# One-core transformer block: query-weight sums one per attention iteration, seventh product half an iteration earlier, GpSimd sums in halves, weight versions loaded ahead

## The chip, the cores and the metric

The kernel runs on one core of a Trainium2 chip. The metric is the device time of one execution in microseconds (us); lower is better. Each run was marked fast or slow; slow is here one more than 1.5% above the fastest of its kernel. Ratios and their 95% intervals use fast runs alone. Kernels that were sent together ran on the same chip, with the kernel before among them. Kernels on different chips are compared by their ratios to the kernel before.

The engines, as the profile names them: PE is TensorE, PEld its weight loads, DVE is VectorE, ACT is ScalarE, POOL is GpSimd, SP is SyncE. A name with a q at its end (ACTq, SPq) is the sequencer of that engine when it issues DMA transfers. L273 is a line of the kernel's source; lines shift by a few between versions of the kernel.

## The reference

One block on 2048 tokens of width 1024: adaptive layer norm, grouped-query attention with 32 query heads of 128 on 512 cached keys, output projection, layer norm again, and a SwiGLU feed-forward part (FFN) of width 3584.

```python
def _A_ref(x, k_cache, v_cache, wq, wo):
    q = (x @ wq).reshape(B, Sq, Hq, Dh) ...          # 32 heads of 128
    k, v = ... the last 512 keys and values, each shared by 8 heads
    p = _softmax(einsum('bhqd,bhkd->bhqk', q, k) * Dh ** -0.5)
    return einsum('bhqk,bhkd->bhqd', p, v) ... @ wo
def _B_ref(x, w_gate, w_up, w_down):
    return _silu(x @ w_gate) * (x @ w_up) @ w_down
mod = _silu(c) @ w_mod                               # six modulation rows
h = _layernorm(x) * (1 + ca) + sa
x = x + ga * _A_ref(h, k_cache, v_cache, wq, wo)
h = _layernorm(x) * (1 + cb) + sb
return x + gb * _B_ref(h, w_gate, w_up, w_down)
```

## The kernel before

The tokens are worked off in two stages of 1024: attention of stage one, its output projection, attention of stage two, its output projection, then the FFN of each stage. The large matrix products are done with a seven-product scheme for 2x2 blocks (seven block products instead of eight). It spares TensorE one eighth of the work and needs sums of weight blocks instead. Three engines share what that brings:

- The sums of the query weights are made on VectorE, four sums of 128x512 for each group of four attention iterations.
- The sums of all other weights are made once, by GpSimd, in 58 "units" (16 for the output projection, 28 for gate and up, 14 for down). A unit loads 512 KB, makes four sums, and writes the result to DRAM. It works in one of two slots of SBUF, at 131 KB and 138 KB.
- The output and down projections later load whole "versions" of their weights, in the order of the seven products. Those loads are issued from ScalarE's queue.

```python
def sum_ops(self, st, eng):              # four sums of one group of weights
    T.op(st, lambda: eng.tensor_tensor(s1, a21, a22, ADD), ...);  yield
    T.op(st, lambda: eng.tensor_tensor(s2, s1, a11, SUB), ...);   yield
    T.op(st, lambda: eng.tensor_tensor(s4, a12, s2, SUB), ...);   yield
    T.op(st, lambda: eng.tensor_tensor(s3, a11, a21, SUB), ...);  yield

def wq_tick(sc, i):
    ...                                  # load of the group's weights
    if (i + 5) % 4 == 0 and 0 <= hp < HP:
        wq_of[sc, hp].sums(DVE, V)       # all four sums, one after the other

def unit_tick(i):                        # GpSimd: one unit every three iterations
    if i % 3 == 0:
        unit_step(OFF_ST if i % NI < NI - 8 else OFF_ST[1:])
```

An attention iteration handles one head and 512 tokens. It has up to two of the seven query products, four score products, two exponentials on ScalarE, and 16 value products, which VectorE evicts from PSUM (L803 takes the reciprocal, L806 multiplies). There are 64 iterations in a stage (`NI`).

```python
def attend(sc, lo, pre, tick):
    hi = (sc + 1) * NI
    for i in range(lo, hi + 2):
        pre(i)
        turn = i % 4 == 2 and group_at(sc, i - 2) >= 0 and i < hi
        if not turn:
            q_first_half(sc, i)
        if lo <= i - 1 < hi:
            scores(i - 1)                # 4 products, 2 exponentials (ACT L784)
        if turn:
            q_first_half(sc, i)          # the fourth product, copied by ACT L1010
        if sc * NI <= i - 2 < hi:
            pv(i - 2)                    # 16 products, eviction DVE L803 and L806
        q_second_half(sc, i)
        tick(i)                          # wq_tick, unit_tick
        ...
        if i == hi - 6:
            start_o(sc)                  # first version of the output weights
        ...
def o_phase(sc, hook):
    load, ver = wo0[sc]
    load(1)                              # second version, after all of attention
    ...
```

The softmax here doesn't subtract the row's maximum and nothing guards it: scores larger than these inputs give would overflow.

## Time and profile before

| | before |
|---|---|
| median, lowest to highest of 4 runs | 1256.13 us, 1253.12 to 1257.26 |
| span of the profiled execution | 1265.0 us |
| PE busy | 1179.5 us, 93% |
| attention iteration, mean of the two loops (24th to 63rd and 65th to 127th eviction) | 3.9 us |
| PE's waits for the eviction L806 | 42.7 us in 21 waits |

From the profile page of the kernel before: the busy time of each engine, the clock that TensorE was granted in 40 slices (in tenths), and the engines of the chain of waits that ended last.

```profile
span 1265.0 us, 18135 instructions
PE 1179.5 (93%) x7087; PEld 589.4 (47%) x7087; DVE 784.5 (62%) x1297; ACT 525.4 (42%) x735; POOL 392.2 (31%) x423
...
PE 79%; DVE 12%; DMA 5%; issue 2%; ACT 2%; POOL 0%; ACTq 0%; DVEq 0%; POOLq 0%
```

TensorE bounds the kernel, and VectorE is the engine that it waits for. The view of waits, for PE of the kernel before, says for what (the line waited for, us in total, number of waits, longest):

```profile
PE ps L273 <- DVE arena L806: 42.7, 21, 5.3
PE ps L273 <- ACT arena L1010: 8.5, 21, 0.5
PE ps L273 <- DMA arena<-in_A_wo_dram: 7.9, 2, 4.2
PE ps L273 <- DMA arena<-in_B_w_down_dram: 5.1, 3, 2.6
```

Nearly two thirds of what is shown is one cause. The view in order of time of the kernel before shows two bursts of the four query-weight sums; the first meets GpSimd sums only from 496.20 on, the second meets one at each. Columns: start, duration, engine, line, operation, output and input, count, and in brackets the idle time before it with what ended it.

```profile
495.15 0.41 DVE L878 TENSOR_TENSOR arena<-arena 128x512 f16<-128x512 bf16 x1
495.60 0.42 DVE L880 TENSOR_TENSOR arena<-arena 128x512 f16<-128x512 f16 x1
...
509.48 1.22 POOL L880 TENSOR_TENSOR arena<-arena 128x512 f16<-128x512 f16 x1
509.72 1.26 DVE L880 TENSOR_TENSOR arena<-arena 128x512 f16<-128x512 f16 x1
...
511.01 2.04 DVE L882 TENSOR_TENSOR arena<-arena 128x512 f16<-128x512 bf16 x1
511.60 1.17 POOL L882 TENSOR_TENSOR arena<-arena 128x512 f16<-128x512 bf16 x1
512.85 1.22 POOL L884 TENSOR_TENSOR arena<-arena 128x512 f16<-128x512 bf16 x1
513.09 1.26 DVE L884 TENSOR_TENSOR arena<-arena 128x512 f16<-128x512 bf16 x1
...
515.07 0.69 DVE L806 TENSOR_TENSOR arena<-ps,rl 128x512 f16<-128x512 f32 x1
...
515.82 4.91 PE L273 MATMUL ps<-arena 128*128 128x129 bf16 x26 [2.50 <-DVE arena L806]
```

The first three sums of the first burst take 0.41 and 0.42 us. The first of the second burst, which begins in the last 0.44 us of a GpSimd sum, takes 0.72 us, and the four that run beside GpSimd sums take 1.26 to 2.04 us (the longest of all 104 takes 3.35 us, L878). The sum begun at 511.01 ends at 513.05, 0.28 us after the GpSimd sum of 511.60 to 512.77. How the two engines hinder each other the trace does not show; it shows the times. The four sums stand in VectorE's queue ahead of the eviction, so the eviction begins at 515.07 and PE has waited 2.50 us. The groups of the kernel before, VectorE's lines by shape, give the mean over all 26 bursts (us busy, mean ns):

```profile
L882 DVE TENSOR_TENSOR arena<-arena 128x512 f16<-128x512 bf16 x26 | 27.9, 1075 | 0.9
L880 DVE TENSOR_TENSOR arena<-arena 128x512 f16<-128x512 f16 x26 | 24.4, 940 | 0.9
...
L884 DVE TENSOR_TENSOR arena<-arena 128x512 f16<-128x512 bf16 x26 | 20.1, 774 | 0.9
L878 DVE TENSOR_TENSOR arena<-arena 128x512 f16<-128x512 bf16 x26 | 17.9, 689 | 0.0
```

That is 90.3 us for 104 sums, 0.87 us each. After a stall the trace also shows a lower clock. The table by stretch of the kernel before (us, then busy time and count of PE, PEld, DVE, ACT and POOL, then the granted clock, the DMA share and GB/s):

```profile
480.00:485.00 5.00, 2.81 (x28) 1.61 (x26) 4.31 (x5) 2.66 (x4) 4.46 (x5) 1.00 0.73 203
485.00:490.00 5.00, 5.00 (x29) 2.32 (x26) 1.56 (x3) 3.17 (x5) 3.66 (x4) 0.66 0.74 193
```

PE idles 2.19 us in the first stretch, in a wait that ends at 484.44, and in the next it is busy all the time at a clock of 0.66, with 29 products instead of the 46 of the stretch after. The 0.66 is an average: the clock stood at 0.50 from 485.57 to 488.99, 3.41 us. The wait of 2.50 us that ends at 515.82 is followed in the same way, by a clock of 0.50 from 516.29 to 519.70. That the low clock comes from the idleness is read from this order and not tested. Seven such pieces lie in the two attention loops of the kernel before (24th to 63rd and 65th to 127th eviction), and each costs up to 1.7 us, so up to 12 us in all (estimates, 3.41 us at half speed).

### The profile page before, as it was taken

How to read it: one execution, taken by the hardware profiler on the slowest of the kernel's cores; microseconds unless marked ns; L12 is line 12 of the kernel's file. 1: busy time of each engine (PE TensorE's matmuls, PEld its weight loads, DVE VectorE, ACT ScalarE, POOL GpSimd, SP SyncE). 2: the span in 40 equal slices, each digit the busy share in tenths (PEclk: the TensorE clock that was granted, in tenths of full speed). 3: DMA queues.
4: the chain of work that ended last, by engine and by line, in shares of the span. 5: the costliest groups of instructions: out<-in, count | busy, mean ns of one | idle time of the engine just before them, and what ended most of it. 6: DMA issues, size and time to landing. Idle time of an engine off the chain costs nothing.

```text
span 1265.0 us, 18135 instructions
## 1 busy us (share of the span) xinstructions
PE 1179.5 (93%) x7087; PEld 589.4 (47%) x7087; DVE 784.5 (62%) x1297; ACT 525.4 (42%) x735; POOL 392.2 (31%) x423
## 2 busy tenths in 40 slices
PE   8798988898998889889889999999999999999998
PEld 5465555453444545445444444444444444444343
DVE  4857776646686776675548766654555654554445
ACT  4475666650105666657620124454401154444110
POOL 1470667533204676775344004443000000000000
PEclk9899999998999999999999999999999999999999
DMA  9786678798845779985789847687397466452453
GB/s 330 190 202 152 177 185 195 170 201 212 248 114 120 180 180 189 207 212 138 179 212 233 237 154 244 215 263 232 115 257 194 138 199 200 152 181 91 160 187 104
DMA packets 305861, 238.71 MB, mean 189 GB/s; under 512 B 132208, under 2 KB 279664, under 8 KB 305776
## 3 DMA queue, kind: packets, MB, share of 16 engines
q1 hardware_dynamic: 234800, 121.67, 39.1%
q0 software_dynamic: 16704, 60.82, 15.9%
q10 hardware_dynamic: 54272, 55.05, 14.3%
q8 instruction: 56, 0.92, 0.3%
q14 instruction: 29, 0.24, 0.1%
HBM read 172.49 MB, written 34.60 MB: 164 GB/s over the span
## 4 chain that ended last, share of the span: by engine, by line
PE 79%; DVE 12%; DMA 5%; issue 2%; ACT 2%; POOL 0%; ACTq 0%; DVEq 0%; POOLq 0%
PE ps L273 78%; DVE arena L806 2%; DMA arena<-in_A_wo_dram 2%; DMA arena<-in_B_w_down_dram 2%; DVE arena L882 2%; DVE arena L880 1%; DVE arena L814 1%; ACT arena L1010 1%; DVE arena L878 1%; ACT arena L784 1%; DVE st L414 1%; DVE arena L594 1%; DVE rl L803 1%; DMA arena<-in_B_w_gate_dram 0%; DVE arena L433 0%
## 5 line engine op out<-in xcount | busy, mean ns | idle before, releaser
L273 PE MATMUL ps<-arena 128*128 128x512 f16 (+3 forms) x6782 | 1172.4, 335 | 80.9 <-DVE arena L806 42.7
L273 PEld LDWEIGHTS ps<-arena 128*128 128x128 bf16 (+1 forms) x6782 | 579.4, 99 | 666.7 <-DVE arena L806 56.0
L784 ACT ACTIVATE arena<-ps 128x1024 bf16<-128x1024 f32 x256 | 261.1, 1022 | 72.4 <-PE ps L273 60.4
L817 ACT ACTIVATE tmp<-ps 128x512 f32<-128x512 f32 x166 | 99.1, 597 | 387.6 <-PE ps L273 332.9
L814 DVE TENSOR_TENSOR arena<-ps,tmp 128x512 bf16<-128x512 f32 (+1 forms) x134 | 91.8, 685 | 59.8 <-PE ps L273 57.1
L814 DVE TENSOR_TENSOR arena<-ps,nsc 128x512 f16<-128x512 f32 x84 | 57.8, 688 | 80.5 <-PE ps L273 68.1
L803 DVE RECIPROCAL rl<-ps 128x4 f32<-128x4 f32 x128 | 23.0, 180 | 122.0 <-PE ps L273 121.5
L806 DVE TENSOR_TENSOR arena<-ps,rl 128x512 f16<-128x512 f32 x128 | 88.5, 691 | 4.9 <-DVE rl L803 0.5
L817 ACT ACTIVATE nsc<-ps 128x512 f32<-128x512 f32 x84 | 50.1, 597 | 96.2 <-PE ps L273 93.8
L1051 DVE TENSOR_TENSOR arena<-arena 128x2048 f16<-128x2048 f16 (+3 forms) x56 | 59.6, 1074 | 18.3 <-PE ps L273 17.7
L419 POOL TENSOR_SCALAR rstd<-mv 128x1 f32<-128x1 f32 x28 | 6.3, 225 | 205.0 <-DVE mv L418 178.8
L1473 ACT ACTIVATE arena<-arena 128x512 f16<-128x512 f16 x84 | 49.8, 624 | 30.7 <-DVE arena L814 30.7
L941 POOL TENSOR_TENSOR arena<-arena 128x512 f16<-128x512 bf16 x30 | 35.8, 1192 | 86.2 <-DMA arena<-in_B_w_down_dram 70.4
L878 POOL TENSOR_TENSOR arena<-arena 128x512 f16<-128x512 bf16 x28 | 34.2, 1220 | 68.9 <-DMA arena<-in_B_w_up_dram 35.1
L817 ACT ACTIVATE arena<-ps 128x512 f32<-128x512 f32 x16 | 9.6, 597 | 90.5 <-PE ps L273 90.5
L814 DVE TENSOR_TENSOR tmp<-ps,tmp 128x512 f32<-128x512 f32 x32 | 22.0, 688 | 38.4 <-ACT tmp L817 28.8
L414 DVE BATCH_NORM_STATS2 st<-x_res 128x6 f32<-128x512 bf16 x62 | 42.3, 682 | 4.0 <-DMA x_res<-in_A_x_dram 3.6
L1490 DVE TENSOR_TENSOR arena<-ps,arena 128x512 f16<-128x512 f32 x28 | 19.4, 692 | 37.1 <-PE ps L273 37.1
L428 DVE TENSOR_SCALAR nsc<-x_res,mv,rstd 128x1024 f16<-128x1024 bf16 (+1 forms) x30 | 20.6, 686 | 29.0 <-DMA arena<-nsc 27.8
L945 POOL TENSOR_TENSOR arena<-arena 128x512 f16<-128x512 bf16 x30 | 37.2, 1241 | 1.5
L943 POOL TENSOR_TENSOR arena<-arena 128x512 f16<-128x512 bf16 x30 | 36.9, 1231 | 2.4
L594 DVE SCALAR_TENSOR_TENSOR arena<-arena 128x1024 bf16<-128x1024 bf16 x24 | 37.5, 1560 | 0.0
(94 smaller groups left out, 700.4 us busy)
## 6 DMA issues: line engine op xcount, KB each, us to landing
arena<-wgu_sum SPq DMA_DIRECT2D x56, 512.0 KB, 6.9
arena<-in_A_wq_dram SPq DMA_DIRECT2D x28, 512.0 KB, 4.8
wgu_sum<-arena POOLq DMA_DIRECT2D x28, 512.0 KB, 3.8
arena<-wo_sum ACTq DMA_DIRECT2D x7, 2048.0 KB, 10.2
arena<-in_B_w_gate_dram SPq DMA_DIRECT2D x28, 512.0 KB, 4.2
arena<-in_B_w_up_dram SPq DMA_DIRECT2D x28, 512.0 KB, 6.4
arena<-wd_sum ACTq DMA_DIRECT2D x8, 1792.0 KB, 8.3
arena<-in_B_w_down_dram ACTq DMA_DIRECT2D x6, 1792.0 KB, 8.3
```

Source lines behind the costliest of these rows:

```text
L273: T.op(PE, lambda: TE.matmul(out_ap, lhsT, rhs, start=start, stop=stop, skip_group_check=skip), reads=reads, writes=[bank_buf])
L414: T.op(DVE, lambda: V.bn_stats(st_[sl][:, hf * 6:hf * 6 + 6], x_res[:, t, hf * 512:hf * 512 + 512]), reads=[B_x[t]], writes=[B_st[sl]])
L594: T.op(DVE, lambda: V.scalar_tensor_tensor(mt[n % 2], mt[n % 2], 1.0, sc_row, op0=ALU.mult, op1=ALU.mult, accum_out=mcol[:, n:n + 1]), rea ...
L784: T.op(ACT, lambda: A.activation(ex_s[es][:, 2 * kp:2 * kp + 2, :], banks2(SCB + 2 * kp), AF.Exp, scale=att_scale), writes=[PB[SCB + 2 * k ...
L806: T.op(DVE, lambda: V.tensor_tensor(o_s[os_].rearrange("p (a b) d -> p a b d", a=2), psap(PVB * 512, [[512, 2], [130, 2], [1, P]]), rlb, A ...
L814: T.op(DVE, lambda: V.tensor_tensor(out, bank(ba), other, ADD), reads=[ob2], writes=[PB[ba], ob])
L817: T.op(ACT, lambda: A.activation(dst, bank(bk), AF.Copy), writes=[PB[bk], db])
L878: T.op(st, lambda: eng.tensor_tensor(s1, a21, a22, ADD), reads=[R, self.b_s3], writes=[self.b_s[0]])
L943: T.op(POOL, lambda: g.tensor_tensor(e[1], b22, e[0], SUB), reads=[R, w.b_s[0]], writes=[w.b_s[1]])
L945: T.op(POOL, lambda: g.tensor_tensor(e[2], b21, e[1], SUB), reads=[R, w.b_s[1]], writes=[w.b_s[2]])
L1051: T.op(DVE, lambda: V.tensor_tensor(o, a, b, SUB), reads=rd, writes=[sb])
L1473: T.op(ACT, lambda: A.activation(o, s_, AF.Silu), reads=[sb], writes=[ob])
```

## The change

Its intent is to take the bursts apart, shorten what VectorE must wait for, and start weight loads before they are missed. In full:

1. The four query-weight sums are made one per iteration.
2. The seventh product moves half an iteration up and takes the place before the scores; the fourth product goes ahead of the scores as well, so its copy on ScalarE stands before the exponentials.
3. GpSimd makes each sum in two halves of 128x256.
4. GpSimd's units come two per five iterations (0.40 an iteration instead of 0.33), and their last ones earlier.
5. The rest of version one and all of version two of the output weights are loaded in the last iteration but one of attention, no longer after it. To have room, they lie partly in GpSimd's two unit slots (131 to 145 KB). The down weights' first versions are loaded one round earlier.
6. Statistics and input loads move to other iterations.

```diff
+def sum_ops(self, st, eng, parts=1):
+    for (o, a, b, op, rd, wr) in (...the four sums...):
+        for h in range(parts):
+            T.op(st, lambda: eng.tensor_tensor(...part h of parts...))
+        yield
 ...                                         # in unit_sums
-    yield from w.sum_ops(POOL, g)
+    yield from w.sum_ops(POOL, g, 2)        # likewise for the other units
 ...
 def q_first_half(sc, i):                    # c = i % 4
-    ...products 3, 2, 4, 5 for c = 0, 1, 2, 3
+    ...products 3, 7, 4, 5
 def q_second_half(sc, i):
-    ...products 7, 1, 6 for c = 1, 2, 3
+    ...products 2, 1, 6
 ...                                         # in wq_tick
-    hp = group_at(sc, i + 5)
-    if (i + 5) % 4 == 0 and 0 <= hp < HP:
-        wq_of[sc, hp].sums(DVE, V)
+    hp = group_at(sc, i + 4 - i % 4)
+    if 0 <= hp < HP and (sc, hp) in wq_of:
+        if i % 4 == 0:
+            sums_of[sc, hp] = wq_of[sc, hp].sum_ops(DVE, V)
+        if (sc, hp) in sums_of:
+            next(sums_of[sc, hp])
 def unit_tick(i):
-    if i % 3 == 0:
-        unit_step(OFF_ST if i % NI < NI - 8 else OFF_ST[1:])
+    if i % 5 in (0, 2):
+        unit_step(OFF_ST if i % NI < NI - 14 else OFF_ST[1:])
 ...                                         # in tick0, likewise in stage two
-    if 6 <= i < NI - 3:
+    if 6 <= i < NI - 8:
         unit_tick(i)
 ...                                         # in start_o
-    places = [[(OFF_WQ, 14), (136 * KB, 2)], [(OFF_E, HP)]] + ...
+    places = [[(OFF_WQ, 14), (131 * KB, 2)], [(133 * KB, 12), (OFF_E, 4)]] + ...
-    wo0[sc][0](0)
+    wo0[sc][0](0, (0,))
 ...                                         # in attend
+    if i == hi - 1:
+        wo0[sc][0](0, (1,))
+        wo0[sc][0](1)
 ...                                         # in o_phase
-    load(1)
 ...                                         # in o_units
-    if j == 1 and (sc or idx % 2 == 0):
+    if j == 1 and idx > 1 and (sc or idx % 2 == 0):
 ...                                         # in the FFN
-    if r == FP - 1:
+    if r == FP - 2:
         ...load(0)
+    if r == FP - 1:
+        load(1)
```

More of the change, by code (lines that the diff above doesn't have):

```diff
@@ L870, in sums @@
                         pass
-                def sum_ops(self, st, eng):
+                def sum_ops(self, st, eng, parts=1):
                     r, (s1, s2, s4) = self.raw, self.s
-                    a11, a12 = r[:, 0:HK, 0:P], r[:, HK:DT, 0:P]
-                    a21, a22 = r[:, 0:HK, P:2 * P], r[:, HK:DT, P:2 * P]
-                    s3 = self.s3
-                    R = self.b_raw
-                    T.op(st, lambda: eng.tensor_tensor(s1, a21, a22, ADD), reads=[R, self.b_s3], writes=[self.b_s[0]])
-                    yield
-                    T.op(st, lambda: eng.tensor_tensor(s2, s1, a11, SUB), reads=[R, self.b_s[0]], writes=[self.b_s[1]])
-                    yield
-                    T.op(st, lambda: eng.tensor_tensor(s4, a12, s2, SUB), reads=[R, self.b_s[1], self.b_s3], writes=[self.b_s[2]])
-                    yield
-                    T.op(st, lambda: eng.tensor_tensor(s3, a11, a21, SUB), reads=[R], writes=[self.b_s3])
-                    yield
+                    R, n = self.b_raw, HK // parts
+                    for (o, a, b, op, rd, wr) in ((s1, (0, P), (HK, P), ADD, [R, self.b_s3], self.b_s[0]),
+                                                  (s2, s1, (0, 0), SUB, [R, self.b_s[0]], self.b_s[1]),
+                                                  (s4, (HK, 0), s2, SUB, [R, self.b_s[1], self.b_s3], self.b_s[2]),
+                                                  (self.s3, (0, 0), (0, P), SUB, [R], self.b_s3)):
+                        for h in range(parts):
+                            x, y = [r[:, z[0] + h * n:z[0] + h * n + n, z[1]:z[1] + P] if type(z) is tuple else z[:, h * n:h * n + n, :]
+                                    for z in (a, b)]
+                            T.op(st, lambda: eng.tensor_tensor(o[:, h * n:h * n + n, :], x, y, op), reads=rd, writes=[wr])
+                        yield
             def seven_at(off, name, kind):
@@ L940, in unit_sums @@
                 R = w.b_raw
-                T.op(POOL, lambda: g.tensor_tensor(e[0], b12, b11, SUB), reads=[R, w.b_s3], writes=[w.b_s[0]])
-                yield
-                T.op(POOL, lambda: g.tensor_tensor(e[1], b22, e[0], SUB), reads=[R, w.b_s[0]], writes=[w.b_s[1]])
-                yield
-                T.op(POOL, lambda: g.tensor_tensor(e[2], b21, e[1], SUB), reads=[R, w.b_s[1]], writes=[w.b_s[2]])
-                yield
-                T.op(POOL, lambda: g.tensor_tensor(rf[:, 1536:2048], b22, b12, SUB), reads=[R], writes=[w.b_s3])
-                yield
+                for (o, a, b, rd, wr) in ((e[0], b12, b11, [R, w.b_s3], w.b_s[0]), (e[1], b22, e[0], [R, w.b_s[0]], w.b_s[1]),
+                                          (e[2], b21, e[1], [R, w.b_s[1]], w.b_s[2]), (rf[:, 1536:2048], b22, b12, [R], w.b_s3)):
+                    for h in range(2):
+                        c = slice(256 * h, 256 * h + 256)
+                        T.op(POOL, lambda: g.tensor_tensor(o[:, c], a[:, c], b[:, c], SUB), reads=rd, writes=[wr])
+                    yield
             def unit_write(k):
@@ L1018, in q_first_half @@
                 c = i % 4
-                if c == 0:
-                    q_step(sc, group_at(sc, i), 3)
-                elif c == 1:
-                    q_step(sc, group_at(sc, i + 3), 2)
-                elif c == 2:
-                    q_step(sc, group_at(sc, i - 2), 4)
+                if c < 3:
+                    q_step(sc, group_at(sc, i - c), (3, 7, 4)[c])
                 else:
@@ L1029, in q_second_half @@
                 c = i % 4
-                if c == 1:
-                    q_step(sc, group_at(sc, i - 1), 7)
-                elif c == 2:
-                    q_step(sc, group_at(sc, i + 2), 1)
-                elif c == 3:
-                    q_step(sc, group_at(sc, i + 1), 6)
+                if c > 0:
+                    q_step(sc, group_at(sc, i + 4 - c), (2, 1, 6)[c - 1])
             ORDER = (1, 2, 6, 5, 3, 7, 4)
@@ L1143, in loader, with load @@
                 got = {}
-                def load(idx):
+                def load(idx, which=None):
                     n = ORDER[idx]
                     dt = BF16 if n < 4 else F16
-                    got[idx], k0 = [], 0
+                    k0 = 0
+                    got.setdefault(idx, [])
                     for q, (off, m) in enumerate(places[idx]):
+                        if which is not None and q not in which:
+                            k0 += m
+                            continue
                         b_ = _Buf("%sv%d_%d_%d" % (kind, sc, idx, q))
@@ L1184, in run_x @@
                         bgx.pop(0)
-            LOADX = {8: 2, 16: 3}
+            LOADX = {6: 2, 12: 3}
             LOADT = {14 + 4 * n: n for n in range(NL)}
@@ L1190, in _ @@
             late = {}
+            sums_of = {}
             def wq_tick(sc, i):
@@ L1256, in pre0 @@
                 mods(i)
-                if i == 20:
+                if i == 14:
                     bg.append(stats_task(2 * TPC, 2 * TPC))
@@ L1270, in start_o @@
                 two = [(103 * KB, 7), (117 * KB, 9)] if sc == 0 else [(OFF_E, HP)]
-                places = [[(OFF_WQ, 14), (136 * KB, 2)], [(OFF_E, HP)]] + [[(o, HP)] for o in (OFF_WQ, OFF_E, OFF_WQ, OFF_N)] + [two]
+                places = [[(OFF_WQ, 14), (131 * KB, 2)], [(133 * KB, 12), (OFF_E, 4)]] + [[(o, HP)] for o in (OFF_WQ, OFF_E, OFF_WQ, OFF_N)] + [two]
                 wo0[sc] = loader(sc, A_wo, wo_sum, HP, "o", places)
-                wo0[sc][0](0)
+                wo0[sc][0](0, (0,))
             def attend(sc, lo, pre, tick):
@@ L1278, in attend @@
                     pre(i)
-                    turn = i % 4 == 2 and group_at(sc, i - 2) >= 0 and i < hi
-                    if not turn:
-                        q_first_half(sc, i)
+                    q_first_half(sc, i)
                     if lo <= i - 1 < hi:
                         scores(i - 1)
-                    if turn:
-                        q_first_half(sc, i)
                     if sc * NI <= i - 2 < hi:
@@ L1292, in attend @@
                         start_o(sc)
+                    if i == hi - 1:
+                        wo0[sc][0](0, (1,))
+                        wo0[sc][0](1)
                     if i >= hi - 1:
                         n = 5 * (i - hi + 1)
-                        o_early(sc, 0, n, n + 5)
-                        o_early(sc, 1, n, n + 5)
+                        for j in range(2):
+                            o_early(sc, j, n, min(n + 5, 14))
             AB_O = (QB, XB, PVB, PVB + 1)
@@ L1316, in o_phase @@
                 load, ver = wo0[sc]
-                load(1)
                 n1 = _N1()
-                b_sj = [_Buf("sj%d" % j) for j in range(TPC)]
-                offs = [(128 + 2 * j) * KB for j in range(TPC)]
-                sj = [(arena.at(offs[j], [CH], F32, [b_sj[j]]), b_sj[j]) for j in range(TPC)]
+                sj = []
                 def rings(tt, j, half):
@@ L1330, in hk @@
                         load(idx + 2)
+                    if j == TPC - 1 and idx == 2:
+                        for n in range(TPC):
+                            b_ = _Buf("sj%d" % n)
+                            sj.append((arena.at((128 + 2 * n) * KB, [CH], F32, [b_]), b_))
                     hook(idx, j)
-                seven_products(HP, oT, B_oT, OFF_OT, n1, ver, AB_O, BB_O, o_out(sc, sj, rings), sj, True, hk, (15, 15, 0, 0))
+                seven_products(HP, oT, B_oT, OFF_OT, n1, ver, AB_O, BB_O, o_out(sc, sj, rings), sj, True, hk, (14, 14, 0, 0))
             def o_units(sc, idx, j):
-                if j == 1 and (sc or idx % 2 == 0):
+                if j == 1 and idx > 1 and (sc or idx % 2 == 0):
                     unit_step(OFF_ST[1:])
@@ L1375, in pre1 @@
             def pre1(i):
-                if i == NI:
+                if i == NI + 46:
                     bg.append(stats_task(0, 2 * TPC))
@@ L1384, in tick1 @@
                     wq_tick(1, i)
-                    if i < 2 * NI - 3:
+                    if i < 2 * NI - 8:
                         unit_tick(i)
@@ L1580, in _ @@
                         load(0)
+                    if r == FP - 1:
+                        load(1)
                 if sc == 0:
                     take_w(FP)
-                load(1)
                 b_sj = [_Buf("fj%d_%d" % (sc, j)) for j in range(TPC)]
```

## The prediction

The forecast's sum: 35 us from attention and 8 to 9 us from the loads, about 44 us, and 1256 less 44 is the 1212 us predicted.

> **What bounds the kernel now.** TensorE. The page gives it 1179.5 of 1265 us busy, and the chain of waits is 79% PE, 12% VectorE, 5% DMA. The stretch table shows where the missing 85 us lie: FFN and output projections run at 93-99% busy; the two attention stages (about 60-282 and 392-643 us) leave 20 and 30 us idle. PE's waits there are mostly for VectorE's attention eviction L806 (15.5 and 21.9 us), which releases the value-product banks. The time-ordered view shows why: once per four iterations VectorE runs the four query-weight sums back to back ahead of that eviction. Each sum takes 0.42 us alone but 1.26 to 2.05 us beside a GpSimd sum (1.15-1.25 us); a burst is 1.7-5.3 us against about 2.5 us of slack. [...]
>
> A second loss: in 5-us stretches that follow such stalls the granted clock is 0.66-0.75 (about eight stretches, estimate 13 us lost). [...]
>
> Elsewhere: each output projection waits 3.7-4.2 us for the second weight version, which can be loaded only when the exponential buffers are free; the down projections wait about 2.5 us twice, and 1 us.
>
> **What the change does.**
> 1. One sum per iteration, after the eviction: no burst, at most 1.3 us between evictions. VectorE has room: 2.6 us an iteration against 3.9. An undisturbed iteration is, by durations in the trace, 1.51 (query products) + 0.86 (scores) + 1.0-1.06 (values) = 3.4 us. Ideal attention: about 30 us less in the second, 18 in the first, clock loss included.
> 2. GpSimd halves: 8 x about 0.6-0.65 us (estimate from half of 1.15 plus a fixed part) instead of 4 x 1.2: [...] VectorE sums average perhaps 0.7 us instead of 0.87.
> 3. Seventh product half an iteration earlier: QB's reader is done before the fourth product, whose ScalarE copy goes ahead of the exponentials; removes the 0.4-us waits for L1010 (8.5 us in all).
> 4. Statistics moved to where VectorE is less loaded.
> 5. Version loads earlier: up to 3.7+4.2 in the output projections and 5-6 us in the FFN, all on the chain.
>
> Ceiling about 50 + 13 = 63 us. I take 70% of attention (35) and 65% of the loads (8-9), about 44 us. Unchanged: the h-sums stall near 111 us (5 us), start (13 us), tail.
>
> **Predicted 1212 us, range 1194 to 1236.** Faster by over 2%: 0.80; within 2%: 0.18; slower: 0.02.
>
> **What would show it.** PE busy share 95-97%; waits for L806 from 42.7 to under 15 us; L878-L884-type VectorE means fall to 0.6-0.75 us; 5-us stretches with clock below 0.8 in attention nearly gone; attention stages near 205-210 and 220-228 us; PE waits for the output and down weights under 5 us together; GpSimd halves 0.55-0.7 us. PE waits on L1010 under 3 us.
>
> **What would make it wrong.** Units come at 0.4 an iteration instead of 0.33, one per 8.6 us, about GpSimd's free pace (8-9 us, 15 with one slot). If it lags, the early load of version two, which needs both unit slots, holds ScalarE's queue before the last exponentials and costs 5-10 us per attention stage. ScalarE (2.7 us an iteration) may become the next limit. In iterations with a modulation column (1.2-1.6 us) VectorE may still be late.

## The result, and the profile after

| | before | change |
|---|---|---|
| median, lowest to highest of 4 runs | 1256.13 us, 1253.12 to 1257.26 | 1220.89 us, 1218.16 to 1225.01 |
| ratio of the fast runs | | 0.9726, 95% interval 0.9694 to 0.9758 |
| span of the profiled execution | 1265.0 us | 1223.2 us |

A ratio is the mean time of one kernel's fast runs over that of the other's fast runs of the same rounds, so it is not quite the ratio of the medians quoted. The change is faster by 35 us of median. The two profiled executions differ by 41.8 us, because that of the kernel before happened to be slower than its median; the ledger below is in those.

The page of the change, the lines that answer to those of before:

```profile
span 1223.2 us, 18300 instructions
PE 1154.5 (94%) x7002; PEld 591.4 (48%) x7087; DVE 735.3 (60%) x1297; ACT 527.9 (43%) x735; POOL 452.8 (37%) x655
...
PE 60%; DMA 16%; POOL 15%; DVE 4%; issue 3%; ACT 1%; ACTq 0%; POOLq 0%; DVEq 0%; SPq 0%
```

VectorE has left the chain (12% to 4%), and GpSimd with its DMA transfers has come onto it: 15% and 16%, where they had 0% and 5%. PE's waits in the change:

```profile
PE ps L273 <- ACT arena L784: 31.0, 5, 18.3
PE ps L273 <- DVE arena L806: 10.7, 2, 5.8
```

The waits for the eviction are down from 42.7 to 10.7 us; those for L1010, the output weights and the down weights are gone. In their place stand 31.0 us of waits for the exponentials L784, where there had been 2.0. Two of the five make up nearly all of it. The groups of the change, by shape, VectorE's query-weight sums and GpSimd's halves:

```profile
L882 DVE TENSOR_TENSOR arena<-arena 128x512 f16<-128x512 bf16 x78 | 42.9, 550 | 0.1
L882 DVE TENSOR_TENSOR arena<-arena 128x512 f16<-128x512 f16 x26 | 13.3, 512 | 0.1
...
L943 POOL TENSOR_TENSOR arena<-arena 128x256 f16<-128x256 bf16 x240 | 176.3, 740 | 92.3 <-DMA arena<-in_B_w_down_dram 70.4 <-DMA arena<-in_A_wo_dram 8.6
```

The 104 sums of VectorE take 56.2 us, 0.54 us each. A half takes GpSimd 0.74 us, so two take 1.48 us where a whole sum took about 1.2.

The table by stretch of the change, same columns as before: a long undisturbed part of attention of stage two, and one stretch at its end.

```profile
390.95:522.19 131.24, 130.19 (x1061) 79.29 (x1080) 86.03 (x173) 102.55 (x121) 91.16 (x124) 1.00 1.02 199
...
595.00:600.00 5.00, 0.00 (x0) 0.00 (x0) 0.00 (x0) 0.00 (x0) 4.52 (x7) 0.50 0.08 28
```

The first covers 40 iterations, 3.28 us each, with PE busy 99% at full clock. In the second nothing runs but GpSimd. Here is the view in order of time of the change at the end of attention of stage one:

```profile
255.41 15.25 ACTq L1144 DMA_DIRECT2D arena<-in_A_wo_dram  x3
...
260.22 5.89 POOL L882 TENSOR_TENSOR arena<-arena 128x256 f16<-128x256 bf16 x8 [5.50 <-DMA arena<-in_B_w_up_dram]
266.40 0.57 POOL L950 DMA_DIRECT2D wgu_sum<-arena  x1 [0.30 <-POOL arena L882]
270.72 2.14 ACT L784 ACTIVATE arena<-ps 128x1024 bf16<-128x1024 f32 x2 [14.38 <-issue]
...
272.91 1.91 PE L273 MATMUL ps<-arena 128*128 128x129 bf16 x16 [10.95 <-ACT arena L784]
```

Read it from the bottom. PE waits 10.95 us for the last two exponentials. These wait 14.38 us, put down to "issue": ScalarE waits for nothing of its own. Ahead of them in its queue are the three loads L1144 that the change put there; they occupy the queue from 255.41 to 270.66, because their place in SBUF is GpSimd's slots, and GpSimd's last unit is summed at 260.22 and its write begins at 266.40. The exponentials begin at 270.72, 0.06 us after the loads have left the queue: here a load that waited for room held the arithmetic behind it. At the end of stage two the same pattern holds PE for 18.34 us (the loads at 593.25 for 12.15 us, the last unit's sums at 595.09, the exponentials at 605.45). There the clock is 0.50 from 591.33 to 611.81.

A ledger, in start times of the eviction L806 (it has one per iteration), before and after:

| part | before, us | change, us | difference |
|---|---|---|---|
| start to 4th eviction | 48.42 | 49.80 | +1.4 |
| 4th to 24th | 79.94 | 83.12 | +3.2 |
| 24th to 63rd | 150.59 | 127.14 | -23.5 |
| 63rd to 64th (end of attention one) | 3.07 | 15.02 | +12.0 |
| 64th to 65th (output projection one) | 111.23 | 106.25 | -5.0 |
| 65th to 127th | 246.99 | 206.07 | -40.9 |
| 127th to 128th (end of attention two) | 3.06 | 22.41 | +19.4 |
| 128th to the end | 621.70 | 613.39 | -8.3 |

The loops of attention give 64 us, and 31 us of these are given back in one iteration at each end. Most of the 64 us can be named: in the loops the waits for L806 went from 34.5 us to none and those for L1010 from 8.5 us to none, and the granted clock rose from 0.98 and 0.97 to 1.00 in both, worth up to 12 us. That is about 55 us; the remaining 9 us are not accounted for.

### The profile page after: what moved, and what is told of

Read it like the earlier page. It is cut to its first block, busy times and chain, and to the rows that moved or that the text cites. A ratio compares the mean times of both kernels' runs of the same rounds, so it can differ in the third digit from the quotient of the medians.

```text
span 1223.2 us, 18300 instructions
## 1 busy us (share of the span) xinstructions
PE 1154.5 (94%) x7002; PEld 591.4 (48%) x7087; DVE 735.3 (60%) x1297; ACT 527.9 (43%) x735; POOL 452.8 (37%) x655
## 4 chain that ended last, share of the span: by engine, by line
PE 60%; DMA 16%; POOL 15%; DVE 4%; issue 3%; ACT 1%; ACTq 0%; POOLq 0%; DVEq 0%; SPq 0%
PE ps L273 60%; POOL arena L882 8%; DMA wgu_sum<-arena 6%; POOL arena L943 4%; DMA arena<-in_B_w_gate_dram 4%; DMA wo_sum<-arena 2%; DMA arena<-in_B_w_up_dram 2%; POOL arena L927 2%; DMA arena<-nsc 1%; DVE arena L433 1%; ACT arena L784 1%; POOL rstd L421 0%; DMA arena<-in_B_w_down_dram 0%; DMA arena<-in_A_wo_dram 0%; DVE x_res L1108 0%
## 5 line engine op out<-in xcount | busy, mean ns | idle before, releaser
L273 PE MATMUL ps<-arena 128*128 128x512 f16 (+2 forms) x6697 | 1146.7, 332 | 64.5 <-ACT arena L784 31.0
L784 ACT ACTIVATE arena<-ps 128x1024 bf16<-128x1024 f32 x256 | 261.4, 1022 | 95.7 <-PE ps L273 47.7
L943 POOL TENSOR_TENSOR arena<-arena 128x256 f16<-128x256 bf16 x240 | 176.3, 740 | 92.3 <-DMA arena<-in_B_w_down_dram 70.4
L882 POOL TENSOR_TENSOR arena<-arena 128x256 f16<-128x256 bf16 x224 | 166.4, 743 | 62.7 <-DMA arena<-in_B_w_gate_dram 28.9
L814 DVE TENSOR_TENSOR arena<-ps,tmp 128x512 bf16<-128x512 f32 (+1 forms) x134 | 91.9, 685 | 56.7 <-PE ps L273 52.6
L814 DVE TENSOR_TENSOR arena<-ps,nsc 128x512 f16<-128x512 f32 x84 | 57.8, 688 | 80.4 <-PE ps L273 68.8
L806 DVE TENSOR_TENSOR arena<-ps,rl 128x512 f16<-128x512 f32 x128 | 88.5, 691 | 4.4
L882 DVE TENSOR_TENSOR arena<-arena 128x512 f16<-128x512 bf16 x104 | 56.2, 540 | 0.2
L814 DVE TENSOR_TENSOR tmp<-ps,tmp 128x512 f32<-128x512 f32 x32 | 22.1, 690 | 54.4 <-ACT tmp L817 45.5
L1487 DVE TENSOR_TENSOR arena<-ps,arena 128x512 f16<-128x512 f32 x28 | 19.4, 692 | 36.7 <-PE ps L273 36.7
L927 POOL DMA_DIRECT2D arena<-in_B_w_down_dram x14 | 11.0, 788 | 72.3 <-DMA wd_sum<-arena 44.6
L1485 DVE TENSOR_TENSOR arena<-arena 128x512 f16<-128x512 f16 x84 | 35.1, 442 | 0.3
L1107 DVE TENSOR_TENSOR tmp<-tmp,rowb 128x512 f32<-128x512 f32 x48 | 33.8, 704 | 1.6
L428 DVE TENSOR_SCALAR nsc<-x_res,mv,rstd 128x1024 f16<-128x1024 bf16 (+1 forms) x30 | 17.8, 594 | 26.8 <-DMA arena<-nsc 25.6
```

What stands on the lines that cost most here:

```text
L273: T.op(PE, lambda: TE.matmul(out_ap, lhsT, rhs, start=start, stop=stop, skip_group_check=skip), reads=reads, writes=[bank_buf])
L784: T.op(ACT, lambda: A.activation(ex_s[es][:, 2 * kp:2 * kp + 2, :], banks2(SCB + 2 * kp), AF.Exp, scale=att_scale), writes=[PB[SCB + 2 * k ...
L806: T.op(DVE, lambda: V.tensor_tensor(o_s[os_].rearrange("p (a b) d -> p a b d", a=2), psap(PVB * 512, [[512, 2], [130, 2], [1, P]]), rlb, A ...
L814: T.op(DVE, lambda: V.tensor_tensor(out, bank(ba), other, ADD), reads=[ob2], writes=[PB[ba], ob])
L882: T.op(st, lambda: eng.tensor_tensor(o[:, h * n:h * n + n, :], x, y, op), reads=rd, writes=[wr])
L927: T.op(Q_of[slot][0], lambda: g.dma_start(dst, src), writes=[w.b_raw, w.b_s3])
```

## The experiments

The questions: where do the 31 us at the ends come from, what brings the 64 us in the loops, and does undoing the loss give a faster kernel? All variants were made from the change unless said otherwise. Twelve kernels ran, and all of them computed the right result.

### late_two: the loads one iteration later

Theory: the loads hold ScalarE's queue, so behind the last exponentials they hold nothing there. Rival: PE would wait as long anyway, as GpSimd is late and the weights are needed next.

```diff
-if i == hi - 1:
+if i == hi:
     wo0[sc][0](0, (1,))
     wo0[sc][0](1)
```

> The changed kernel with the early weight loads issued one iteration later, behind the last exponentials in ScalarE's queue. Theory L (the load of version two cannot start before GpSimd's last unit has been written out, whichever instruction queue holds it): the idle of 11 and 18 us in front of the last value products turns into a PE wait for the output weights of about the same size; 1214 to 1222 us against 1221 for the change. Rival Q (what costs is only the order in ScalarE's queue): the idle goes away; 1190 to 1202 us.

Measured: 1216.1 us (1204.8 to 1223.8, the last of these slow; before 1261.8, ratio 0.9612 [0.9528, 0.9696]; this chip was noisy, 1250.6 to 1268.9 for the kernel before). PE's waits:

```profile
PE ps L273 <- DMA arena<-in_A_wo_dram: 21.3, 3, 12.2
```

The exponentials no longer wait, and PE waits 21.3 us for the output weights instead (4.51, 4.51 and 12.23 us). So the place in the queue explains in which form the wait appears, and 8 us of its size (the two stalls were 29.3 us together); most of it remains, because the slots come free late.

### units_short: GpSimd's units end earlier

The rest of the theory: GpSimd is behind. Here its last units of each attention stage are left out and made in the output projections.

```diff
-unit_step(OFF_ST if i % NI < NI - 14 else OFF_ST[1:])
+unit_step(OFF_ST if i % NI < NI - 17 else OFF_ST[1:])
-if 6 <= i < NI - 8:                     # stage two: i < 2 * NI - 8
+if 6 <= i < NI - 14:                    # stage two: i < 2 * NI - 13
-if j == 1 and idx > 1 and (sc or idx % 2 == 0):
+if j == 1 and idx > 1:
```

> The changed kernel with the last GpSimd units of each attention stage moved to later stages (the stage's last unit at its iteration 47 and 48 instead of 55 and 53; five units move to the output projections and the FFN). Theory L: both unit slots are free when the early load is issued, so the idle of 11 and 18 us and the low clock after it go, 1186 to 1197 us. Rival (the early loads cost at that place for another reason, such as DMA contention or the work on the slots' bytes): at most 8 us gained, 1212 or more.

Measured: 1211.05 us (1207 to 1225), ratio 0.9622 [0.9541, 0.9703]. The stalls at both ends of attention are gone, so GpSimd's units were their cause. But the gain I expected did not come. A new wait stands in the first down projection, in the view in order of time of this run:

```profile
868.84 5.83 POOL L943 TENSOR_TENSOR arena<-arena 128x256 f16<-128x256 bf16 x8 [3.62 <-DMA arena<-in_B_w_down_dram]
...
874.97 0.57 POOL L950 DMA_DIRECT2D wd_sum<-arena  x1 [0.30 <-POOL arena L943]
877.91 0.37 ACTq L1144 DMA_DIRECT2D arena<-wd_sum  x1
...
885.82 5.50 PE L273 MATMUL ps<-arena 128*128 128x512 f16 x18 [9.06 <-DVE tmp L814]
```

GpSimd finishes its last unit of the down weights at 874.97, the load of those sums is issued at 877.91, and PE stands still for 9.06 us. The profile names the VectorE line that ended last. That the late unit is the true cause is read from this order and not tested by itself. Another 4.15 us end at 355.40, in the output projection. GpSimd's work is conserved: units not made in attention have to be made where PE may wait for them too.

### whole_sums: GpSimd's sums undivided

Is it the halving that makes GpSimd late?

```diff
-yield from w.sum_ops(POOL, g, 2)
+yield from w.sum_ops(POOL, g)
-for h in range(2):
-    c = slice(256 * h, 256 * h + 256)
+for h in range(1):
+    c = slice(0, 512)
```

> The changed kernel with GpSimd's sums undivided, nothing else. Theory L with the halves as a cause of GpSimd's lag: a unit takes about 4.8 us of sums instead of 5.9 and comes every 8.3 to 8.8 us instead of 9.4 to 10.0; the stall in the second attention stage falls from 18 to under 10 us; 1203 to 1217 us, while VectorE's sums rise from 0.54 to about 0.65 us. Rival (the halves are what keeps VectorE in time): waits for L806-type evictions come back, 1225 us or more.

Measured: 1211.44 us (1204 to 1223; without the slow run the highest is 1218), ratio 0.9605 [0.9498, 0.9712]. There is no stall at either end. A unit takes 9.1 us in attention of stage two (issue of one write to that of the next, 19 intervals) and took 10.0 us in the change, against a demand of one per 2.5 iterations, which is 2.5 x 3.28 = 8.2 us. When only one slot is left, the last units of stage one take 14.9 and 14.7 us instead of 17.5 and 18.5. But in attention of stage one, the groups of four from the 21st to the 41st eviction take 3.8 to 4.5 us an iteration, and its 63rd eviction is 14 us later than the change's. In stage two most groups take 3.28 us an iteration, as with halves, though VectorE's sums rose to 0.79 us each, more than the 0.65 us that I expected. So halving helps in stage one, where VectorE has statistics and modulation columns besides, and only delays GpSimd in stage two.

### old_loads: the output projection's loads as before

```diff
-places = [[(OFF_WQ, 14), (131 * KB, 2)], [(133 * KB, 12), (OFF_E, 4)]] + ...
+places = [[(OFF_WQ, 14), (136 * KB, 2)], [(OFF_E, HP)]] + ...
-wo0[sc][0](0, (0,))
+wo0[sc][0](0)
-if i == hi - 1:
-    wo0[sc][0](0, (1,))
-    wo0[sc][0](1)
 ...                                     # load(1) back at the start of o_phase
```

> The changed kernel with the output projection's version loads and their places as before the change (the FFN's early loads stay). Theory L: no wait for the unit slots, the idle of 11 and 18 us goes, and a wait for the output weights of about 4 us per projection comes back; 1194 to 1207 us. Rival (the loss at the end of attention has another cause than the early load): 1214 or more.

Measured: 1214.34 us (1205 to 1221.5), ratio 0.9623 [0.9546, 0.97]. The last iterations run freely, but the first version's second piece lies in a unit slot here as well and is issued six iterations before the end: a stall of 7.92 us that ends at 571.12, and waits of 2.40 and 2.68 us for the second version come back. The time is outside what I expected and at the rival's edge: moving the loads back does not remove the stall. Here too a load into a slot that GpSimd still used stalled ScalarE.

These four shared one noisy chip; their ratios' intervals overlap, so their order among each other is not settled. What they show is in their traces.

### after_again: the change once more, as a control

It ran on a second chip in five rounds, together with the next three kernels. No edit.

> The changed kernel, word for word, as the control for the runs beside it. Both theories: ratio to before 0.965 to 0.976, with ScalarE held before the last exponentials of both attention stages by 10 to 20 us in the profile.

Measured: 1219.48 us (1215 to 1228.4), ratio 0.9705 [0.9666, 0.9743], before 1258.5; stalls of 10.67 and 13.88 us at the two ends. The result and its stalls repeat.

### spread_only: the kernel before, with its sums spread

The one part alone. The kernel before gets the new `wq_tick` and nothing else.

> The kernel before with one part of the change alone: each query-weight sum in an iteration of its own. Theory S (the burst of sums was the cause of the attention stalls): PE waits for L806 fall from 43 us to under 15, an iteration of the second attention takes 3.3 to 3.4 us, the output weights are still waited for (about 4 us per projection); 1206 to 1220 us where before takes 1256. Rival (the seventh product's move and the halved GpSimd sums are needed for it): less than half of that, 1232 us or more.

Measured: 1230.09 us (1225 to 1231.5), ratio 0.9775 [0.9741, 0.9809]. PE's waits:

```profile
PE ps L273 <- DVE arena L806: 12.1, 5, 6.4
PE ps L273 <- ACT arena L1010: 8.6, 22, 0.4
```

Those for L806 were 42.7 us before; those for L1010 are still there. The iteration is 3.45 us in most of the loops. That lies between my expectation and its rival, nearer the rival: spreading alone is worth 28 us, three quarters of the change's 37 us (1 - 0.9775 against 1 - 0.9705). The interval excludes no gain, but not a gain of just under 2%.

### best: halves where they help, fewer units at the ends

The four first runs point to this: halves only for the output projection's units, which are made in the first part of stage one, and stage one's units cut as in units_short.

```diff
+n_h = 2 if units[k][0] == "o" else 1
-for h in range(2):
-    c = slice(256 * h, 256 * h + 256)
+for h in range(n_h):
+    c = slice(512 // n_h * h, 512 // n_h * (h + 1))
 ...                                     # "g" units: w.sum_ops(POOL, g)
-if 6 <= i < NI - 8:
+if 6 <= i < NI - 14:                    # stage one only; one slot from NI - 17 there
-if j == 1 and idx > 1 and (sc or idx % 2 == 0):
+if j == 1 and idx > 1:
```

> The changed kernel with GpSimd's lag taken away without losing units late in the FFN: halves kept for the 16 output-weight units alone, the rest undivided; three units of the first attention stage moved, two of them to the first output projection. Theory L: no wait of ScalarE for a unit slot at the end of either attention stage (each idle in front of the last value products under 2 us), attention iterations of 3.3 us kept; 25 to 32 us below the changed kernel beside it, 1190 to 1198 us. Rival (the idle only moves to a later stage, as in the run with short unit lists): under 12 us gained.

Measured: 1203.71 us (1194.4 to 1211.3), ratio 0.9559 [0.9515, 0.9603]. That is 16 us under the change, and less than I expected. Both end stalls are gone but 1.78 us. A new wait stands at the end of output projection one, in the view in order of time of this run:

```profile
346.69 7.27 POOL L882 TENSOR_TENSOR arena<-arena 128x512 f16<-128x512 bf16 x4 [3.84 <-DMA arena<-in_B_w_gate_dram]
347.39 2.18 DVE L829 TENSOR_TENSOR arena<-arena 128x2048 f16<-128x2048 f16 x1
349.49 2.17 DVE L830 TENSOR_TENSOR arena<-arena 128x2048 f16<-128x2048 f16 x1
351.58 3.57 DVE L882 TENSOR_TENSOR arena<-arena 128x512 f16<-128x512 bf16 x4
...
357.23 1.01 PE L273 MATMUL ps<-arena 128*128 128x512 f16 x2 [6.12 <-DVE arena L1102]
```

It is the slowdown of the bursts again, between other parties. A GpSimd unit put into the projection runs beside VectorE's sums of the next stage's inputs (2.18 us each; the two begun before the unit took 1.22) and beside a burst of four query-weight sums (3.57 us, 0.89 each). Each side slows the other: GpSimd's four sums take 7.27 us, where an undisturbed one takes about 1.2. VectorE comes late to its next eviction, L1102, and PE waits 6.12 us.

### best_late: best, with the loads one iteration later

```diff
-if i == hi - 1:
+if i == hi:
```

> The same, and the early loads issued behind the last exponentials (one iteration later). Theory L: where the slots are free in time the place in the queue matters little; within 4 us of the run beside it, with a wait for the output weights of 0 to 4 us per projection. Rival Q (the place in ScalarE's queue matters by itself): over 6 us faster than the run beside it.

Measured: 1204.17 us (1199 to 1208), ratio 0.9569 [0.9536, 0.9603]. It is the same as best. Once GpSimd is out of the slots, the loads' place in the queue costs nothing that can be measured. For the exponentials to be held, both have to be there: the slot still in use and the load queued before them. With the slot in use alone PE still waits, for the weights (21.3 us in late_two).

### best_seven_back: best, with the seventh and fourth product back

On another chip, five rounds, with the next three (before 1259.99). best itself was not run there, so these four are set against it by the two ratios to the kernel before; the intervals of two ratios together leave 7 to 8 us either way on each such difference. The two functions `q_first_half` and `q_second_half` and `turn` in `attend` are those of the kernel before.

> The best version so far with the seventh product and the fourth put back where they stood before the change. Theory S (the move removes the PE wait for ScalarE's copy and the uneven spacing): an iteration of the second attention grows from 3.28 us to 3.4 to 3.5 us, the 0.4-us waits for the copy at L1010 come back (about 9 us in all), 10 to 18 us slower than the best version, 1213 to 1222 us. Rival (the move is worth only those 9 us at most, since the spread sums already leave slack): under 6 us slower.

Measured: 1217.13 us (1211 to 1219), ratio 0.9656 [0.962, 0.9692], against 0.9559 for best: some 12 us slower. PE's waits for the fourth product's copy are back, at L1007 here:

```profile
PE ps L273 <- ACT arena L1007: 9.4, 22, 0.7
```

The iteration is 3.45 us again instead of 3.28, the same as in spread_only. So the move is worth about 12 us, give or take 7, and the waits shown are 9.4 us.

### best_burst: best, with the four sums in a burst

```diff
-hp = group_at(sc, i + 4 - i % 4)
-if 0 <= hp < HP and (sc, hp) in wq_of:
-    ...one sum per iteration
+hp = group_at(sc, i + 5)
+if (i + 5) % 4 == 0 and 0 <= hp < HP:
+    wq_of[sc, hp].sums(DVE, V)
```

> The best version with the four query-weight sums in one burst every fourth iteration, as before the change. Theory S: PE waits for L806 come back at 1 to 3 us per group, iteration 3.6 to 3.9 us, 25 to 45 us slower than the best version, 1228 to 1248 us. Rival (with the undivided sums and the seventh product moved the burst fits in the slack): under 10 us slower.

Measured: 1242.14 us (1227.7 to 1245), ratio 0.9844 [0.9797, 0.9891], some 36 us slower than best. PE's waits:

```profile
PE ps L273 <- DVE arena L814: 31.9, 23, 4.6
```

The size is as expected. The waiter's name is not: with the products in their new order, what stands behind the burst is the addition that makes a query (L814) and no longer the eviction L806.

### best_whole: best, with no halves at all

```diff
-n_h = 2 if units[k][0] == "o" else 1
+n_h = 1
```

> The best version with no GpSimd sum halved at all. Theory H (halves pay only where statistics, column sums and query sums meet on VectorE, about iterations 24 to 44 of the first attention): those iterations take 3.7 to 4.0 us instead of 3.28, 8 to 15 us slower than the best version, the second attention unchanged at 3.28 us. Rival (halves are worth nothing): within 4 us.

Measured: 1217.82 us (1212.6 to 1225.5), ratio 0.9673 [0.9634, 0.9713], some 14 us slower than best. Most of the loss has one place: the 24th to the 40th eviction take 65.4 us (4.1 us an iteration), in best 52.5 us (3.3 us). In stage two most groups take 3.28 us an iteration in both (209.6 us for the loop, in best 207.4), but a stall of 4.22 us for L784 is back at its end.

### best_idx: best, with no unit at the end of projection one

This tests the reading of best's new wait: leave the last two products of that projection without a unit, and give attention one more.

```diff
-if 6 <= i < NI - 14:
+if 6 <= i < NI - 12:
-if j == 1 and idx > 1:
+if j == 1 and idx > 1 and (sc or idx < 5):
```

> The best version with no GpSimd unit in the last two products of the first output projection, where five VectorE sums of one kind follow each other, and one unit more left in the attention stage. Theory K (the 6 to 8.6-us wait for VectorE at the end of that projection comes from GpSimd's sums [...]): that wait falls under 3 us and nothing else moves; 3 to 7 us faster than the best version, 1196 to 1201 us. Rival: the wait stays.

Measured: 1197.9 us (1192.6 to 1204.7), ratio 0.9516 [0.9474, 0.9557]. This is the lowest ratio of all, though its interval overlaps that of best. From its page and from its waits:

```profile
PE 1156.6 (97%) x7087; PEld 587.9 (49%) x7087; DVE 761.9 (64%) x1297; ACT 527.7 (44%) x735; POOL 410.8 (34%) x487
```

```profile
PE ps L273 <- DVE arena L1102: 1.8, 1, 1.8
```

The wait of 6.1 us is down to 1.8 us, and no single wait of that size took its place, which supports the reading. But something else did move: the loop of stage two takes 211.7 us, in best 207.4. Against the change the ratios give 0.9516 / 0.9705 = 0.98, two per cent, across two chips, so it is less firm. VectorE's sums average 0.69 us here ((57.1 + 14.6) us for 104), more than the change's 0.54, and in stage one the iteration is still 3.28 us from the 25th eviction on. In stage two eight of 15 groups of four take 3.33 to 3.73 us an iteration, where the change has three above 3.28, and the loop takes 5.6 us more than the change's 206.1: with the sums spread, longer sums cost little there, but not nothing.

Not tried: the moved statistics and input loads alone, the earlier down-weight loads alone, and a GpSimd pace of one unit per three iterations with everything else of the change.

## Why the prediction was right or wrong

Faster by over 2% and the range held: predicted 1212 us, range 1194 to 1236, measured 1220.89. The sum was 44 us of gain, 35 from attention and 8 to 9 from loads. It came out 9 us too good, and behind that stand two larger errors that partly cancel: the loops gave more than was counted, and the ends of attention lost what was not counted at all. That the total fell inside the range is partly luck.

**What bounds the kernel, and the bursts: right.** Waits for L806 were to fall from 42.7 to under 15 us and fell to 10.7. spread_only shows this to be the largest single part, 28 us; best_burst shows it from the other side, 36 us lost, though the wait then had another name.

**The gain of the attention loops: too small.** The ideal was put at 48 us, of which 70% were counted; the loops gave 64 us (23.5 + 40.9 in the ledger). The ideal iteration was taken as 3.4 us; it is 3.28 us. The seventh product's move was sized by the 8.5 us of waits that the profile showed and is worth about 12 us (best_seven_back). The waits for L1010 were to be under 3 us and are gone.

**GpSimd's halves: wrong in size.** The estimate was 0.60 to 0.65 us for a half; it took 0.74 us on average, and 0.67 us where no VectorE operation between SBUF tiles ran beside it (1.15 us for a whole sum). A half begins 0.75 us after the one before it, a whole sum about 1.23 us after; so by these two spacings a sum made in two halves takes about 2 x 0.75 - 1.23 = 0.27 us longer than a whole one (an estimate). VectorE's sums became shorter than forecast (0.54 us mean, forecast 0.6 to 0.75), and that was of no use once they were spread, except in the middle of stage one, where most of the 14 us lost in best_whole lies.

**The step that failed: the early load.** The prediction named it as what would make it wrong, in the words "If it lags, the early load of version two, which needs both unit slots, holds ScalarE's queue before the last exponentials and costs 5-10 us per attention stage", and put nothing of it into the sum. GpSimd did lag: 9.35 and 10.0 us a unit (11 and 18 intervals) against a demand of 8.2 us, where the estimate of its free pace had been 8 to 9 us; with one slot 17.5 and 18.5 us, where the estimate was 15. The cost was 12.0 and 19.4 us in the ledger, of which 10.95 and 18.34 us are waits for the exponentials. The mechanism was as described; its chance and its size were both taken too small. Demand followed from the change itself: attention became faster, so 0.40 units an iteration meant one per 8.2 us, and halves made each unit slower (10.0 us against 9.1 in whole_sums). The trace of the kernel before already had 9.4 us a unit in stage two (18 intervals from 404.54 to 573.05), above the 8 to 9 us of the estimate. These numbers could have been set side by side before the run.

In the kernel before, GpSimd was not behind. Its units are not tied to the iterations of the loop; GpSimd runs ahead as far as loads and slots allow. Of its 19 units of attention one the last is written from here, 30 us before the last eviction at 282.02:

```profile
252.45 0.57 POOL L954 DMA_DIRECT2D wgu_sum<-arena  x1 [0.30 <-POOL arena L884]
```

The writes after it, at 266.69 and 285.67, are of units of the output projection, and they cost nothing, because nothing in ScalarE's queue needed their slot. In the change the last of 20 units is written at 266.40, and the 63rd eviction now comes at 260.06. GpSimd had one unit more to make, it worked with a single slot for longer (two intervals of 17.5 and 18.5 us, before one of 15.5), and attention ended earlier. Work that had been in time became a stall when a load into its place was put before work that PE needs.

**The loads: too small.** The waits for output and down weights were to fall from 13.0 to under 5 us and are gone. The stages that hold them became 5.0 and 8.3 us shorter, 13 us where 8 to 9 were counted. How much of this comes from the earlier loads was not tried by itself.

**The marks in the profile.** PE's busy share was to be 95 to 97% and is 94%; in best_idx, with the ends repaired, it is 97%. Attention stages were to take 205 to 210 and 220 to 228 us; counted alike (60 us to the 64th eviction, 65th to 128th) they took 215 and 228 us, with the end stalls in them. Stretches with a low clock inside attention were to be nearly gone: in the 131 us shown above the clock is 1.00, and most of the low clock is now in the stalls at the ends (0.50 from 267.06 to 277.30 and from 591.33 to 611.81; outside them it is 0.50 from 58.85 to 65.68 and from 120.29 to 123.70).

**Still open.** The iteration's gain from 3.45 to 3.28 us (0.17 us x some 104 iterations is 17 us), the 9.4 us of waits and the timed loss of 12 us in best_seven_back all agree within the 7 us of noise, so whether the move does more than remove those waits is not shown. The two waits for L806 that end near 60 and 120 us (the start, and the sums of the inputs) were 5.25 and 2.89 us before and are 5.76 and 4.96 us in the change; no variant removes them. A wait of 3.85 us that ends at 693.16, at the end of output projection two, is put down to "issue"; the kernel before does not have it, most variants do (2.8 to 5.2 us), and its cause was not looked for. Whether the order of the four first variants is real, the noise of their chip does not say.

## What to carry to other kernels

Spread work that stands ahead of an eviction over the iterations, before shortening its pieces: once spread, longer sums cost little here in most of attention (VectorE's took 0.79 us in whole_sums instead of 0.54, and most groups of stage two stayed at 3.28 us an iteration), while the halves made their engine slower (10.0 us a unit instead of 9.1). Before loading something earlier, ask which engine's queue will hold the load (here ScalarE's, for 15.25 and 12.15 us), what must leave the place it goes to, and at what pace that leaves under the new, faster loop. Work of a second engine that is put off does not go away; it has to be put where neither TensorE nor the engine that it slows is in a hurry (in best it slowed VectorE's sums from 1.22 to 2.18 us, and PE waited 6.12 us).
